# Attention of a pair in two-bank tiles, and seven products for all of batches 1 to 3

## The chip, the cores and the metric

One core of a Trainium2 chip runs the whole program in one launch. The metric is device time in microseconds (us). Engines: TensorE (PE, and PEld for its weight loads), VectorE (DVE), ScalarE (ACT), GpSimd (POOL), and SyncE (SP), whose queue issues most DMAs.

## What is computed

```python
# q, k, v: (B, H, S, D) = (4, 8, 768, 64); n_global 8, n_local 96
scores = q @ k.T / sqrt(D)
keep   = (pos_k < 8) | ((0 <= rel) & (rel < 96))        # rel = pos_q - pos_k
dist   = 96 for a global key out of the window, else |rel|
scores = where(keep, scores - slope[h] * dist, -1e9)    # slope[h] = 2 ** -(h + 1)
x      = softmax(scores) @ v                            # heads side by side: (4, 768, 512)
u      = x + (U @ V) applied along the sequence         # rank 32; U 768x32, V 32x768
out    = u + relu(u @ w_ch1) @ w_ch2                    # 512 -> 2048 -> 512
```

The slope of a head is half that of the head before it.

## The kernel before

A step `i` handles one pair of heads: `b = i // 4` is the batch, `i % 4` the pair, 16 steps in all. The instructions stand in the order in which the program writes them (a manual schedule), so every engine works off its own queue in that order.

**Attention of a pair.** Per 128 queries only their own 128 keys count (`kT`), and the 128 before with the 8 global keys patched in (`kA`). The 11 blocks of a head lie side by side, 1408 columns, made in three chunks of 512, 512 and 384 (`st_S(i, c)`, scores at L360 and L367). For batch 0 a matmul adds the bias (L352) and ScalarE takes the exponential from PSUM (`st_SE`, L379). From batch 1 on VectorE adds the bias table `relcat`, one step a head and chunk (`s_dve`, L392), from PSUM into `sp`, and ScalarE takes one exponential a head (`st_E`, L404). `st_V` multiplies by `v` (L416, L420) into the PSUM tile `ob`; VectorE takes the reciprocal of the sums (L425) and normalizes (L439); GpSimd casts to fp16 into `x16` (L440).

**Low-rank step.** `st_M1` (L449) projects `x16` on U, VectorE copies (L453); `st_MT` turns it (L466), VectorE copies it to `tmp16` (L467); `st_M3` multiplies by V (L503) in two halves of three matmuls, in an `sc` bank and in `ob`; VectorE adds each half to `x_sb` (L508), GpSimd casts the whole (L512), and `st_X` has a DMA transpose it to `uT`. Batch 0 does the add by `st_M2` instead (copies at L485 and L487).

**Feed-forward.** A batch has three groups of 256 tokens. A group has 8 *up* units of 8 matmuls of 256 columns (L609), each with a ReLU into `htr` (L614). Then a plain group has 8 *down* units of 4 matmuls of 512 columns (L639), with an add to `x_sb` and a store after each four (L644). A group in `WG` does the down projection as a 2 x 2 block product by seven block products instead of eight: units x1 to x4 in PSUM tile `cx` and y1 to y3 in `cy`, each 8 matmuls of 256 columns (L659) and a VectorE add to `x_sb` (L664). For these VectorE makes sums s1 to s4 of blocks of `htr`, in two parts each, and once sums t1 to t4 of blocks of `w_ch2` (L540). The sums wait in the list `jobs`; one is taken off after each unit, and `need` takes off what a product lacks, in order, just before it.

**Order.** A first loop (i = 0 to 3) does attention of batch 0. The second loop's passes, called slots here by their `i` (4 to 17), put feed-forward units between the pieces of attention: the tuple `units` says how many stand at each of nine places. In order: chunk 0 of pair i, 1st place, `st_V(i-1, 0)` and (i < 7) the transposes of the next pair (`st_T`, L250, kT copied at L273), 2nd, chunk 1, 3rd, `st_V(i-1, 1)`, 4th, chunk 2, 5th, `st_M1(i-1)` and the first exponential, 6th, `st_MT(i-1)` and the next pair's kA (`st_K`, L335, L336), 7th, `st_M3(i-1, 0)` and the second exponential, 8th, `st_M3(i-1, 1)` and `st_X`, 9th. Chunk 0 of slot 4 stands ahead of the loop, among the last steps of batch 0. What units are left after slot 17 run by themselves: the tail. In slots 4 to 6 the units are batch 0's ups; GpSimd also makes kA there (L290), casts v (L136), copies vA (L299) and issues weight DMAs (L222, L225).

PSUM has eight banks: two single-bank `sc` tiles, one `ob`, two `cps` (also `cx`, `cy`), three `th` (ups, transposes).

Of the kernel before, what the change touches and what calls it, by code (L numbers as in the profile page):

```python
# [20 lines left out]
def kernel(  # L21
# [46 lines left out]
    WG = ((2, 1), (2, 2), (3, 0), (3, 1), (3, 2))  # L68
# [11 lines left out]
    def ps_sc(tag="sc"):  # L80
        return psum.tile([P, 512], FP32, name="sc", tag=tag, bufs=2)
# [84 lines left out]
    setup = scp.tile([P, 384], I32, name="setup", tag="ep0")  # L166
# [16 lines left out]
    relcat = cst.tile([P, 640], FP32, name="relcat")  # L183
# [17 lines left out]
    for vt in vbuf:  # L201
        nc.gpsimd.memset(vt[:, :, :, D:D + 1], 1.0)
    nc.gpsimd.tensor_copy(relcat[:, 0:512].rearrange("p (a c) -> p a c", a=2), rel3[:, 0:2])
    nc.gpsimd.tensor_copy(relcat[:, 512:640], relB[:, 0:P])
    finish_table(
        relcat, relcat[0:NG, 0:512].rearrange("p (a c) -> p a c", a=2)[:, :, P:]
    )
# [22 lines left out]
    def new_batch(b):  # L230
        xs[b] = xp.tile([P, NSB, DM], FP32, name="x_sb", tag="x_sb", bufs=3)
        x16s[b] = xp.tile([P, NP, NSB, P], FP16, name="x16", tag="x16")
        tmps[b] = xp.tile([P, DM], FP16, name="tmp16", tag="tmp16", bufs=3)
        uTs[b] = xp.tile([P, NDC, S], FP16, name="uT", tag="uT")
# [97 lines left out]
    def st_K(i):  # L332
        kT = kts[i]
        kA = kp.tile([P, NSB - 1, P], FP16, name="kA", tag="kA")
        nc.vector.tensor_copy(kA.rearrange("d n p -> d (n p)"), kT[:, 0:S - P])  # L335
        nc.vector.tensor_copy(  # L336
            kA[:, 1:, 0:NG], kT[:, 0:NG].unsqueeze(1).broadcast_to((P, NSB - 2, NG))
        )
        kas[i] = kA
# [3 lines left out]
    def scores(i, c, on_pe):  # L343

        kT, kA, qT = kts[i], kas[i], qts[i]
        c0 = 512 * c
        tot = min(512, W - c0)
        r0 = 256 if c else 0
        scs = [ps_sc("cps" if on_pe and (i + c) % 2 else "sc") for hi in range(2)]
        if on_pe:  # L350
            for hi in range(2):
                nc.tensor.matmul(  # L352
                    scs[hi][:, 0:tot], slI[:, 2 * (i % NP) + hi],
                    rel16.rearrange("p a c -> p (a c)")[:, r0:r0 + tot], start=True, stop=False,
                )
        for kb in (2 * c, 2 * c + 1):
            o = 256 * kb - c0
            for hi in range(2):
                r = slice(hi * D, (hi + 1) * D)
                nc.tensor.matmul(  # L360
                    scs[hi][:, o:o + P], kT[r, kb * P:(kb + 1) * P], qT[r, kb * P:(kb + 1) * P],
                    start=(o == 0 and not on_pe), stop=(o + P == tot),
                )
# [7 lines left out]
        return [(sc, c0, tot, r0) for sc in scs]  # L371

    def st_SE(i, c):

        if c == 0:
            for hi in range(2):
                eps[i, hi] = scp.tile([P, W], FP16, name=f"ep{hi}", tag=f"ep{hi}")
        for hi, (sc, c0, tot, _) in enumerate(scores(i, c, True)):
            nc.scalar.activation(  # L379
                eps[i, hi][:, c0:c0 + tot], sc[:, 0:tot], AF.Exp, scale=qk_scale  # L380
            )

    relfs = (relcat[:, 0:512], relcat[:, 256:512].unsqueeze(1).broadcast_to((P, 2, 256)), relcat[:, 256:640])

    def s_dve(i, hi, got):
        sc, c0, tot, r0 = got
        if c0 == 0:
            sps[i, hi] = scp.tile([P, W], FP32, name=f"sp{hi}", tag=f"sp{hi}", bufs=1)
        dst, got = sps[i, hi][:, c0:c0 + tot], sc[:, 0:tot]
        if c0 == 512:  # L390
            dst, got = (t.rearrange("p (a c) -> p a c", a=2) for t in (dst, got))
        nc.vector.scalar_tensor_tensor(  # L392
            out=dst, in0=got,
            scalar=qk_scale / slope[2 * (i % NP) + hi], in1=relfs[c0 // 512],
            op0=ALU.mult, op1=ALU.add,
        )

    def st_S(i, c):
        for hi, got in enumerate(scores(i, c, False)):
            s_dve(i, hi, got)  # L400

    def st_E(i, hi):
        ep = scp.tile([P, W], FP16, name=f"ep{hi}", tag=f"ep{hi}")
        nc.scalar.activation(  # L404
            ep, sps.pop((i, hi)), AF.Exp, scale=slope[2 * (i % NP) + hi]
        )
        eps[i, hi] = ep

    def st_V(i, hi):
        b, h = i // NP, 2 * (i % NP) + hi  # L410
        ep, vt, vA = eps.pop((i, hi)), vts[i], vas[i]
# [15 lines left out]
        x16 = x16s[b][:, i % NP, :, hi * D:(hi + 1) * D]  # L427
# [12 lines left out]
        nc.gpsimd.tensor_copy(x16, xo)  # L440


    def st_M1(i):
        b, dc = i // NP, i % NP
        ch = slice(dc * P, (dc + 1) * P)
        if b:
            tps = ps_ob()
            for n in range(NSB):
                nc.tensor.matmul(  # L449
                    tps[:, 0:R], x16s[b][:, dc, n], u16[:, n, 0:R],  # L450
# [5 lines left out]
        for n in range(NSB):  # L456
            nc.tensor.matmul(
                tps[:, 0:P], u16[:, n], x16s[b][:, dc, n],
# [10 lines left out]
    def st_M2(i):  # L469
        b, dc = i // NP, i % NP  # L470
        ch = slice(dc * P, (dc + 1) * P)
        for g in range(2):
# [5 lines left out]
            for t in range(NTG):  # L478
                nc.tensor.matmul(
                    ups[:, t * P:(t + 1) * P], x16s[b][:, dc, NTG * g + t], ident16,  # L480
# [9 lines left out]
    def st_X(i):  # L490
# [3 lines left out]
            x16s[b][:, dc].rearrange("p n d -> p (n d)"),  # L494
        )

    def st_M3(i, g):
        b, dc = i // NP, i % NP
        ch = slice(dc * P, (dc + 1) * P)
        ups = ps_ob() if g else ps_sc()  # L500
        for t in range(NTG):
            n = NTG * g + t
            nc.tensor.matmul(  # L503
                ups[:, t * P:(t + 1) * P], v16w[:, n * P:(n + 1) * P], tmps[b][:, ch],
                start=(t == 0), stop=(t == NTG - 1),
            )
        dst = xs[b][:, NTG * g:NTG * (g + 1), ch]
        nc.vector.tensor_tensor(  # L508
            dst, ups[:, 0:GT].rearrange("p (t d) -> p t d", t=NTG), dst, ALU.add
        )  # L510
        if g == 1:
            nc.gpsimd.tensor_copy(x16s[b][:, dc], xs[b][:, :, ch])  # L512
# [23 lines left out]
    have = set()  # L536

    def queue_sum(name, part, out_, a, b_, op):
# [35 lines left out]
    def queue_group(b, g):  # L574
# [9 lines left out]
        def queue_sums(k):  # L584

            h = cell["htr"]
            if k == 0:
                for x in range(1, 5):
                    cell[f"s{x}"] = ffp.tile([P, HJ, P], FP16, name=f"s{x}", tag=f"s{x}", bufs=1)
                cell.update(a11=h[:, 0:HJ, 0:P], a12=h[:, HJ:NJC, 0:P],  # L590
                            a21=h[:, 0:HJ, P:FT], a22=h[:, HJ:NJC, P:FT])
            js = slice(k * HJ // 2, (k + 1) * HJ // 2)
            for name, a, b_, op in (
# [3 lines left out]
                queue_sum((name, b, g), k, cell[name][:, js], cell[a][:, js], cell[b_][:, js], op)  # L597
# [76 lines left out]
        if split:  # L674
# [7 lines left out]
            for made in (x1, y1, x2, y2, x3, y3, x4) if last else (x1, y1, y2, x2, y3, x3, x4):  # L682
# [8 lines left out]
    def fill(n):  # L691
        for _ in range(n):
            unit()
            if jobs:
                jobs.popleft()()
# [22 lines left out]
    for i in range(NP):  # L718
# [34 lines left out]
        if i == 2:  # L753
            load_w1(1)
        st_SE(i, 2)
# [19 lines left out]
    for i in range(NP, NPAIR + 2):  # L775
# [65 lines left out]
        if i > NP:  # L841
            st_M3(i - 1, 0)
# [3 lines left out]
        if i > NP:  # L846
            st_M3(i - 1, 1)
# [45 lines left out]
```

## Time and profile before

| | |
|---|---|
| median of 3 runs (lowest, highest) | 233.26 us (233.09, 233.36) |
| the profiled execution: its time, its span | 233.38 us, 231.4 us |
| granted TensorE clock | 0.999 |
| matmuls of plain downs (L639), of products (L659) | 224, 280 |
| bias steps of VectorE (L392), 128x512 and 128x384 | 48 and 24 |

The span runs from the first to the last instruction that the profile holds; 2.0 us of the time lie outside it. In windows, an engine's busy time is the union of its instructions' records. Matmul records overlap, since matmuls are pipelined: the time of a row of them is read from one start to the next. Slots 4 to 15 begin, at the first scores of chunk 0, at 27.4, 39.5, 50.5, 60.7, 72.4, 83.9, 96.2, 108.4, 120.4, 132.4, 144.4 and 156.5 us; the tail begins near 180.

### The profile page before, as it was taken

The numbers are of one execution on the slowest core, as the hardware profiler recorded it, in microseconds if no ns is written. First come the engines' busy times: TensorE is split into PE (matmuls) and PEld (weight loads), VectorE is DVE, ScalarE is ACT, GpSimd is POOL, SyncE is SP. The second block draws the span as 40 slices with busy tenths as digits, with TensorE's granted clock in tenths as the row PEclk, the third lists the DMA queues.
The fourth block names the chain that finished last, engine by engine and source line by source line (L and its number), as shares of the span: only waits on it lengthen the run. The fifth ranks groups of instructions, "written<-read, shape, count | busy, mean of one in ns | idle before, by whom it ended". The sixth has DMA issues, their size and how long they took to land.

```text
span 231.4 us, 5678 instructions
## 1 busy us (share of the span) xinstructions
PE 223.6 (97%) x2324; PEld 161.5 (70%) x2324; DVE 150.4 (65%) x350; ACT 111.3 (48%) x167; POOL 80.5 (35%) x131
## 2 busy tenths in 40 slices
PE   7999999999999999999999999999999999999994
PEld 2455678778644457766666756866688888888883
DVE  3787794868577767566657675779895524444452
ACT  6776948685722222927263707473533334333320
POOL 6399736668344243332415051503120100000000
PEclk9999999999999999999999999999999999999999
DMA  6999999999999997987695965542131302011112
GB/s 194 308 287 248 253 215 244 307 178 139 226 204 279 215 259 181 225 180 198 147 235 121 259 152 145 144 103 79 32 81 48 79 3 91 1 48 45 45 48 91
DMA packets 86561, 36.66 MB, mean 158 GB/s; under 512 B 74152, under 2 KB 83592, under 8 KB 86536
## 3 DMA queue, kind: packets, MB, share of 16 engines
q1 hardware_dynamic: 81480, 32.01, 54.5%
q0 software_dynamic: 5056, 4.29, 12.8%
q8 instruction: 18, 0.29, 0.6%
q14 instruction: 7, 0.06, 0.1%
HBM read 27.46 MB, written 6.29 MB: 146 GB/s over the span
## 4 chain that ended last, share of the span: by engine, by line
PE 83%; POOL 5%; DMA 3%; DVE 3%; ACT 2%; issue 1%; SPq 1%; POOLq 0%
PE hps L609 33%; PE cps L639 22%; PE cx L659 8%; PE cy L659 5%; PE sc L360 3%; DMA vst<-in_v_dram 3%; PE ob L420 2%; PE ob L416 2%; PE sc L367 1%; ACT ep L404 1%; POOL v L136 1%; PE sc L503 1%; ACT htr L614 1%; PE ob L503 1%; PE tp L250 1%
## 5 line engine op out<-in xcount | busy, mean ns | idle before, releaser
L614 ACT ACTIVATE htr<-hps 128x512 f16<-128x512 f32 x96 | 56.8, 598 | 85.3 <-PE hps L609 82.4
L609 PE MATMUL hps<-uT,w 128*128 128x256 f16 x756 | 96.2, 273 | 0.5 <-DVE uT L485 0.3
L609 PEld LDWEIGHTS <-w 128*128 128x128 f16 x756 | 70.5, 98 | 11.3 <-issue 0.4
L639 PE MATMUL cps<-w,htr 128*128 128x512 f16 x224 | 56.9, 379 | 0.0
L392 DVE SCALAR_TENSOR_TENSOR sp<-sc,relcat 128x512 f32<-128x512 f32 (+1 forms) x72 | 43.2, 640 | 17.6 <-PE sc L360 8.9
L404 ACT ACTIVATE ep<-sp 128x1408 f16<-128x1408 f32 x24 | 32.7, 1372 | 16.3 <-DVE sp L392 16.3
L512 POOL CAST x<-x_sb 128x768 f16<-128x768 f32 x12 | 10.3, 856 | 61.9 <-DVE x_sb L508 61.9
L639 PEld LDWEIGHTS <-htr 128*128 128x128 f16 x224 | 19.1, 97 | 16.6
L440 POOL CAST x<-x_sb 128x384 f16<-128x384 f32 x30 | 15.8, 526 | 25.8 <-DVE x_sb L439 25.6
L360 PEld LDWEIGHTS <-kT 64*128 64x128 f16 x192 | 8.2, 93 | 15.1 <-issue 13.5
L540 DVE TENSOR_TENSOR s<-htr 128x512 f16<-128x512 f16 x20 | 9.3, 463 | 12.7 <-ACT htr L614 12.7
L439 DVE TENSOR_TENSOR x_sb<-ob,rcp 128x384 f32<-128x384 f32 x30 | 16.7, 557 | 1.0
L659 PEld LDWEIGHTS <-s 128*128 128x128 f16 x160 | 15.5, 98 | 1.8
L360 PE MATMUL sc<-qT,kT 64*128 64x128 f16 x192 | 16.8, 221 | 0.0
L420 PE MATMUL ob<-v,ep 128*128 128x65 f16 x192 | 16.5, 193 | 0.0
L420 PEld LDWEIGHTS <-ep 128*128 128x128 f16 x192 | 13.9, 98 | 3.0 <-ACT ep L379 0.3
L664 DVE TENSOR_TENSOR x_sb<-cx,x_sb 128x256 f32<-128x256 f32 x20 | 8.4, 422 | 10.1 <-PE cx L659 10.0
L416 PE MATMUL ob<-vA,ep 128*128 128x65 f16 x160 | 14.4, 194 | 0.4 <-DVE vA L312 0.2
L136 POOL CAST v<-vst 128x768 f16<-128x768 f32 x16 | 13.5, 842 | 3.6 <-DMA vst<-in_v_dram 3.6
L367 PE MATMUL sc<-qT,kA 64*128 64x128 f16 x160 | 14.2, 217 | 0.4 <-DVE kA L286 0.2
L379 ACT ACTIVATE ep<-sc 128x512 f16<-128x512 f32 (+1 forms) x24 | 12.1, 559 | 4.4 <-PE sc L367 4.1
L659 PEld LDWEIGHTS <-htr 128*128 128x128 f16 x120 | 11.7, 98 | 1.3
(102 smaller groups left out, 265.7 us busy)
## 6 DMA issues: line engine op xcount, KB each, us to landing
qst<-in_q_dram SPq DMA_DIRECT2D x16, 384.0 KB, 4.7
kst<-in_k_dram SPq DMA_DIRECT2D x16, 384.0 KB, 6.7
vst<-in_v_dram SPq DMA_DIRECT2D x16, 384.0 KB, 3.8
out_dram<-x_sb SPq DMA_DIRECT2D x23, 256.0 KB, 2.3
w<-in_moe_w_ch_dram POOLq DMA_DIRECT2D x8, 512.0 KB, 8.0
vA<-v SPq DMA_DIRECT2D x8, 152.3 KB, 4.4
out_dram<-x_sb SPq DMA_DIRECT2D x2, 128.0 KB, 1.7
uT<-x SPq DMA_TRANSPOSE x12, 2.8
```

What stands on the lines that cost most here:

```text
L136: nc.gpsimd.tensor_copy(vt.rearrange("p n h d -> p h n d")[:, :, :, 0:D], vsts.pop(i).rearrange("p (h n) d -> p h n d", h=2),)
L360: nc.tensor.matmul(scs[hi][:, o:o + P], kT[r, kb * P:(kb + 1) * P], qT[r, kb * P:(kb + 1) * P], start=(o == 0 and not on_pe), stop=(o + P ...
L367: nc.tensor.matmul(scs[hi][:, o + P:o + 2 * P], kA[r, kb], qT[r, (kb + 1) * P:(kb + 2) * P], start=False, stop=(o + 2 * P == tot),)
L392: nc.vector.scalar_tensor_tensor(out=dst, in0=got, scalar=qk_scale / slope[2 * (i % NP) + hi], in1=relfs[c0 // 512], op0=ALU.mult, op1=ALU ...
L404: nc.scalar.activation(ep, sps.pop((i, hi)), AF.Exp, scale=slope[2 * (i % NP) + hi])
L416: nc.tensor.matmul(ob[:, qi], ep[:, OF[qi - 1]:OF[qi - 1] + P], vA[:, qi - 1, hi], start=True, stop=False,)
L420: nc.tensor.matmul(ob[:, qi], ep[:, DG[qi]:DG[qi] + P], vt[:, qi, hi], start=(qi == 0), stop=True,)
L439: nc.vector.tensor_tensor(xo, ob[:, :, 0:D], rb, ALU.mult)
L609: nc.tensor.matmul(hps[:, k * FT:(k + 1) * FT], w1_16[:, dc, jt * P:(jt + 1) * P], uT[:, dc, ts], start=(dc == 0 and k == 0), stop=(dc == ...
L614: nc.scalar.activation(cell["htr"][:, 2 * jp:2 * jp + 2].rearrange("p j t -> p (j t)"), hps, AF.Relu)
L639: nc.tensor.matmul(cps, htr[:, jc, t * P:(t + 1) * P], w2_16[:, jc], start=(b > 0 and jc == 0), stop=(jc == NJC - 1),)
L659: nc.tensor.matmul(ps, cell[a][:, j], tw[w][:, j], start=(first and j == 0), stop=(done is not None and j == HJ - 1), skip_group_check=True,)
```

## The change

- `WG` holds all nine groups of batches 1 to 3 (five before). The products of every group stand in the order x1, y1, x2, y2, x3, y3, x4, so `cx` and `cy` take turns.
- The `sc` tile is one tile of two banks, one copy: a bank a head. VectorE's bias step covers both heads in one instruction: the table `relcat2` holds the table and its half, and the scale is that of the pair's first head. `sp` and `ep` are pair tiles. In batch 0 every second chunk has one exponential for both heads, the others use two `cps` tiles. `st_R` makes the half table in pass 2 of the first loop.
- `st_M3` is one block of six matmuls in the two banks of `sc`, with one VectorE add.
- Chunk 0's bias step of slot 4 is issued after the last `st_M2` of batch 0; before, its two steps stood between the pieces ahead of it.
- The large part of the kA copy (L335 before) goes to ScalarE.
- s3 is made in place of a block of `htr`. The weight sums t1, t2, t4 have a buffer of their own and start in group (0, 1). Every sum carries a count of units before which it isn't taken off the list; `need` ignores the count.
- `units`: slots 4 to 6 move the unit of the 3rd place to the 9th (8 units as before); slots 7 and 8 have 9 instead of 10, slots 9 to 17 10 instead of 11.

```diff
-    WG = ((2, 1), (2, 2), (3, 0), (3, 1), (3, 2))
+    WG = tuple((b, g) for b in range(1, B) for g in range(NFG))
...
-    def ps_sc(tag="sc"):
-        return psum.tile([P, 512], FP32, name="sc", tag=tag, bufs=2)
+    def ps_sc():
+        return psum.tile([P, 2, 512], FP32, name="sc", tag="sc", bufs=1)
...
-        nc.vector.tensor_copy(kA.rearrange("d n p -> d (n p)"), kT[:, 0:S - P])
+        nc.scalar.copy(kA[:, :, NG:], kT.rearrange("d (n p) -> d n p", n=NSB)[:, 0:NSB - 1, NG:])
...
-        scs = [ps_sc("cps" if on_pe and (i + c) % 2 else "sc") for hi in range(2)]
+        both = None if on_pe and (i + c) % 2 else ps_sc()
+        scs = [ps_cps("sc") if both is None else both[:, hi] for hi in range(2)]
...
+    def st_R():
+        nc.vector.tensor_scalar_mul(relcat2[:, 1], relcat, 0.5)
+    relfs = (relcat2[:, :, 0:512], relcat2[:, :, 256:768], relcat2[:, :, 256:640])
...
         nc.vector.scalar_tensor_tensor(
-            out=dst, in0=got,
-            scalar=qk_scale / slope[2 * (i % NP) + hi], in1=relfs[c0 // 512],
+            out=sps[i][:, :, c0:c0 + tot], in0=both[:, :, 0:tot],
+            scalar=qk_scale / slope[2 * (i % NP)], in1=relfs[c0 // 512],
             op0=ALU.mult, op1=ALU.add,
         )
...
-    def st_M3(i, g):
-        ups = ps_ob() if g else ps_sc()
+    def st_M3(i):
+        ups = ps_sc()
...
-    def queue_sum(name, part, out_, a, b_, op):
+    def queue_sum(name, part, out_, a, b_, op, wait=0):
...
-        jobs.append(go)
+        jobs.append((count[0] + wait, go))
...
-        t = xp.tile([P, 3, HJ, HD], FP16, name="t16", tag="x_sb", bufs=3)
+        t = wbig.tile([P, 3, HJ, HD], FP16, name="t16")
...
-                queue_sum(name, k, tw[name][:, js], a[:, js], b_[:, js], ALU.subtract)
+                queue_sum(name, k, tw[name][:, js], a[:, js], b_[:, js], ALU.subtract, wait=4 * len(jobs))
...
-                            a21=h[:, 0:HJ, P:FT], a22=h[:, HJ:NJC, P:FT])
+                            a21=h[:, 0:HJ, P:FT], s3=h[:, 0:HJ, P:FT], a22=h[:, HJ:NJC, P:FT])
...
-                queue_sum((name, b, g), k, cell[name][:, js], cell[a][:, js], cell[b_][:, js], op)
+                queue_sum((name, b, g), k, cell[name][:, js], cell[a][:, js], cell[b_][:, js], op, wait=0 if last else 2)
...
-                if (t, part) == (0, 1) and not split and follow in WG:
+                if (t, part) == (0, 1) and (b, g) == (0, NFG - 2):
                     queue_weight_sums()
...
-            for made in (x1, y1, x2, y2, x3, y3, x4) if last else (x1, y1, y2, x2, y3, x3, x4):
+            for made in (x1, y1, x2, y2, x3, y3, x4):
...
     def fill(n):
         for _ in range(n):
             unit()
-            if jobs:
-                jobs.popleft()()
+            count[0] += 1
+            if jobs and jobs[0][0] < count[0]:
+                jobs.popleft()[1]()
...
     st_M2(NP - 2)
-    s_dve(NP, 0, first[0])
     begin_up(0, (0, 1), ps_cps("hps"))
     st_M1(NP - 1)
-    s_dve(NP, 1, first[1])
     begin_up(0, (2,))
     begin_up(1, (0, 1, 2), ps_th("hps"))
     st_M2(NP - 1)
+    s_dve(NP, first)
...
-            (1, 1, 1, 1, 1, 1, 1, 1, 0) if i + 1 < NPE
-            else (1, 1, 1, 2, 1, 1, 1, 1, 1) if i < 2 * NP + 1
-            else (2, 1, 1, 2, 1, 1, 1, 1, 1)
+            (1, 1, 0, 1, 1, 1, 1, 1, 1) if i + 1 < NPE
+            else (1, 1, 1, 1, 1, 1, 1, 1, 1) if i < 2 * NP + 1
+            else (1, 1, 1, 2, 1, 1, 1, 1, 1)
```

More of the change, by code (lines that the diff above doesn't have):

```diff
@@ L165 @@
     warm(8)
-    setup = scp.tile([P, 384], I32, name="setup", tag="ep0")
+    setup = scp.tile([P, 384], I32, name="setup", tag="ep")
     reli = setup[:, 0:256]
@@ L182 @@
     nc.vector.tensor_copy(ident16, ident)
-    relcat = cst.tile([P, 640], FP32, name="relcat")
+    relcat2 = cst.tile([P, 2, 768], FP32, name="relcat")
+    relcat = relcat2[:, 0]
     rel16 = cst.tile([P, 3, 256], BF16, name="rel16")
@@ L202 @@
         nc.gpsimd.memset(vt[:, :, :, D:D + 1], 1.0)
[L203 to L207, printed above, removed]
+    relcat3 = relcat.rearrange("p (a c) -> p a c", a=3)
+    nc.gpsimd.tensor_copy(relcat3, rel3)
+    finish_table(relcat, relcat3[0:NG, :, P:])
     def load_uv():
@@ L370, in scores, with s_dve @@
                     )
-        return [(sc, c0, tot, r0) for sc in scs]
+        return scs, both, c0, tot
     def st_SE(i, c):
         if c == 0:
-            for hi in range(2):
-                eps[i, hi] = scp.tile([P, W], FP16, name=f"ep{hi}", tag=f"ep{hi}")
-        for hi, (sc, c0, tot, _) in enumerate(scores(i, c, True)):
+            eps[i] = scp.tile([P, 2, W], FP16, name="ep", tag="ep")
+        scs, both, c0, tot = scores(i, c, True)
+        if both is not None:
             nc.scalar.activation(
-                eps[i, hi][:, c0:c0 + tot], sc[:, 0:tot], AF.Exp, scale=qk_scale
+                eps[i][:, :, c0:c0 + tot], both[:, :, 0:tot], AF.Exp, scale=qk_scale
             )
-    relfs = (relcat[:, 0:512], relcat[:, 256:512].unsqueeze(1).broadcast_to((P, 2, 256)), relcat[:, 256:640])
-    def s_dve(i, hi, got):
-        sc, c0, tot, r0 = got
+            return
+        for hi, sc in enumerate(scs):
+            nc.scalar.activation(
+                eps[i][:, hi, c0:c0 + tot], sc[:, 0:tot], AF.Exp, scale=qk_scale
+            )
+    def st_R():
+        nc.vector.tensor_scalar_mul(relcat2[:, 1], relcat, 0.5)
+    relfs = (relcat2[:, :, 0:512], relcat2[:, :, 256:768], relcat2[:, :, 256:640])
+    def s_dve(i, got):
+        _, both, c0, tot = got
         if c0 == 0:
[L388 to L391, printed above, removed]
+            sps[i] = scp.tile([P, 2, W], FP32, name="sp", tag="sp", bufs=1)
         nc.vector.scalar_tensor_tensor(
-            out=dst, in0=got,
-            scalar=qk_scale / slope[2 * (i % NP) + hi], in1=relfs[c0 // 512],
+            out=sps[i][:, :, c0:c0 + tot], in0=both[:, :, 0:tot],
+            scalar=qk_scale / slope[2 * (i % NP)], in1=relfs[c0 // 512],
             op0=ALU.mult, op1=ALU.add,
@@ L398, in st_S @@
     def st_S(i, c):
-        for hi, got in enumerate(scores(i, c, False)):
-            s_dve(i, hi, got)
+        s_dve(i, scores(i, c, False))
     def st_E(i, hi):
-        ep = scp.tile([P, W], FP16, name=f"ep{hi}", tag=f"ep{hi}")
+        if hi == 0:
+            eps[i] = scp.tile([P, 2, W], FP16, name="ep", tag="ep")
         nc.scalar.activation(
-            ep, sps.pop((i, hi)), AF.Exp, scale=slope[2 * (i % NP) + hi]
+            eps[i][:, hi], sps[i][:, hi], AF.Exp, scale=slope[2 * (i % NP)]
         )
-        eps[i, hi] = ep
     def st_V(i, hi):
         b, h = i // NP, 2 * (i % NP) + hi
-        ep, vt, vA = eps.pop((i, hi)), vts[i], vas[i]
+        ep, vt, vA = eps[i][:, hi], vts[i], vas[i]
+        if hi == 0:
+            x16s[i] = xp.tile([P, NSB, P], FP16, name="x16", tag="x16", bufs=3)
         obf = ps_cps("ob") if (i, hi) == (NP - 1, 1) else ps_ob()
@@ L426, in st_V @@
         xo = xs[b][:, :, h * D:(h + 1) * D]
-        x16 = x16s[b][:, i % NP, :, hi * D:(hi + 1) * D]
+        x16 = x16s[i][:, :, hi * D:(hi + 1) * D]
         rb = rcp.unsqueeze(2).broadcast_to((P, NSB, D))
@@ L493, in st_X @@
             uTs[b][:, dc].rearrange("d (n p) -> d n p", n=NSB),
[L494 removed]
+            x16s[i].rearrange("p n d -> p (n d)"),
         )
[L497 removed]
+    def st_M3(i):
         b, dc = i // NP, i % NP
         ch = slice(dc * P, (dc + 1) * P)
[L500 to L502 removed]
+        ups = ps_sc()
+        for n in range(NSB):
+            g, t = divmod(n, NTG)
             nc.tensor.matmul(
[L504 removed]
+                ups[:, g, t * P:(t + 1) * P], v16w[:, n * P:(n + 1) * P], tmps[b][:, ch],
                 start=(t == 0), stop=(t == NTG - 1),
             )
[L507 removed]
+        dst = xs[b][:, :, ch].rearrange("p (g t) d -> p g t d", g=2)
         nc.vector.tensor_tensor(
[L509 removed]
+            dst, ups[:, :, 0:GT].rearrange("p g (t d) -> p g t d", t=NTG), dst, ALU.add
         )
[L511 to L512 removed]
+        nc.gpsimd.tensor_copy(x16s[i], xs[b][:, :, ch])
     ups_q, downs_q = deque(), deque()
@@ L754 @@
             load_w1(1)
+            st_R()
         st_SE(i, 2)
@@ L841 @@
         if i > NP:
-            st_M3(i - 1, 0)
+            st_M3(i - 1)
         if live:
@@ L846 @@
         if i > NP:
-            st_M3(i - 1, 1)
             st_X(i - 1)
```

14 lines of the change are left out of this document (7 added, 7 removed).

## The prediction

> **What bounds the kernel now.** I read the page first, then busy time in windows (one per slot, from the first scores of one slot to those of the next), the chain of waits in order of time, and the timeline around the places that the change touches. A lane is an engine's queue, which it works off in order.
>
> ```profile
> PE 223.6 (97%) x2324; PEld 161.5 (70%) x2324; DVE 150.4 (65%) x350; ACT 111.3 (48%) x167; POOL 80.5 (35%) x131
> ```
> ```profile
> 39.51:50.54 11.03, 10.61 (x135) 8.60 (x135) 7.37 (x15) 8.49 (x13) 7.61 (x12) 1.00 1.15 247
> 108.41:120.41 12.00, 12.00 (x122) 7.83 (x121) 7.79 (x17) 6.19 (x8) 4.16 (x7) 1.00 0.74 173
> 156.47:167.50 11.03, 11.03 (x118) 7.42 (x118) 10.06 (x23) 5.01 (x7) 3.21 (x4) 1.00 0.22 58
> ```
> After the stretch and its length come busy PE, PEld, DVE, ACT and POOL. TensorE is busy throughout in slot 11 and in slot 15 up to its `st_M3` (second and third line), at full clock. VectorE has 4.2 us to spare in slot 11, but 1.0 us in slot 15, where weight sums and the first product sums fall. So TensorE's work is the time, unless a wait is put into its lane.
>
> ```profile
> 84.65 1.73 PE cps L639 x8
> ```
> ```profile
> 224.57 0.87 PE cy L659 x8
> 225.45 0.87 PE cx L659 x8
> ```
> From the chain: eight 512-column matmuls of a plain down take 1.73 us (0.216 each); eight 256-column matmuls of a product take 0.87 (0.109 each).
>
> **A. Four more groups by seven products.** A plain group's down projection is 32 x 0.216 = 6.92 us, one by products 7 x 0.87 = 6.11: 0.8 saved. The order in which the changed program stands has 504 product matmuls against 280 and 96 plain ones against 224, so four groups: **-3.2**. All of it is on TensorE, which sets the end. Fewer units in a slot only move units to the tail, where the same lane does them.
>
> The Trainium skill ("TensorE: Matmul & The Clock Gate", Back-to-back issue gap) gives 81 ns for a 128-column and 131 ns for a 512-column matmul in a stream with weight loads. By that a plain unit would be 4 x 0.131 = 0.52 and, estimated at about 0.1 per 256 columns, a product 0.8, so that the four groups would cost about 6 us instead of saving 3. The 0.216 and 0.109 above disagree, and the sum goes by them.
>
> **B. Slots 4 to 6: the bias step of a pair.** Before, a head's step (L392) frees its own bank. Now one step covers both banks of the only `sc` tile, so the next scores wait for all of it. Its size: 512 columns take 0.684 and 384 take 0.551 (mean of the groups), 1.04 ns a column, so 1024 take 0.684 + 0.53 = 1.22 and 768 take 0.95 (ends: 0.68, one step, and 1.37, two). Steps in a row overlap by some 0.08.
>
> ```profile
> 31.43 0.56 DVE L485 CAST uT<-ups 128x384 f16<-128x384 f32 x1 [0.22 <-PE ups L479]
> 31.90 1.01 DVE L772 TENSOR_TENSOR x_sb<-ob,rcp 128x384 f32<-128x384 f32 x2
> 33.13 0.96 DVE L273 COPY kT<-tp 128x768 f16<-128x768 f16 x1 [0.21 <-PE tp L250]
> 34.00 1.28 DVE L392 SCALAR_TENSOR_TENSOR sp<-sc,relcat 128x512 f32<-128x512 f32 x2
> ```
> ```profile
> 33.79 1.91 PE L609 MATMUL hps<-uT,w 128*128 128x256 f16 x16 [0.16 <-ACT qT L272]
> 35.63 0.23 PE L360 MATMUL sc<-qT,kT 64*128 64x128 f16 x2
> ```
> Slot 4, timeline of before. Chunk 0's two steps ran at 29.74 and 30.54, ahead of the last uT copy. The change issues its one step behind that copy, from 31.90. Queued behind it on VectorE: two L772 (0.93), kT (0.87), then chunk 1's step: 31.90 + 1.13 + 0.93 + 0.87 = 34.83, done 36.05. TensorE waits for it: between scores 1 and 2 there is now one unit, not two (33.79 + 0.97 = 34.76). Scores 2 start at 36.1: a wait of **1.3**.
>
> ```profile
> 45.11 0.85 POOL L136 CAST v<-vst 128x768 f16<-128x768 f32 x1
> 46.03 0.73 POOL L299 COPY vA<-v 128x650 f16<-128x650 f16 x1
> 46.70 0.51 POOL L440 CAST x<-x_sb 128x384 f16<-128x384 f32 x1
> ```
> ```profile
> 47.27 0.22 PEld L449 LDWEIGHTS <-x 128*128 128x128 f16 x6 [0.62 <-POOL x L440]
> ```
> Slots 5 and 6: `st_M1` needs GpSimd's second x16 cast, which stands behind kA (43.44), a weight DMA, v and vA, some 3.8 us from kT's end. TensorE already waits 0.5 there in slot 5. ScalarE's second exponential ends near 41.65 by the shift; the pair's chunk-0 step, whose output tile both exponentials read, follows at 41.7, then two steps and kT (to 44.5); the cast ends 1.1 later than before. TensorE arrives a unit (0.87) earlier in its slot, so 1.1 + 0.87 = 2.0 lost by the end of slot 5, that is 0.6 beyond slot 4. In slot 6, where the cast ended (57.06) only 0.34 ahead of its reader, 0.87 - 0.34 = 0.5 and 0.1 at scores 2: 0.6. B is **+2.5**; ends 0.7 (the waits of 0.5 and 0.4 that slot 5 has now absorb the shift) and 3.2.
>
> **C. The first group of batch 1, slot 10.** There its first s1, s2, s4, s3 and the last weight sums meet. TensorE's order is six low-rank matmuls, product x2 (t2 by s2), up; VectorE's is the low-rank add (`st_M3`), s1, s2, and x2's fifth weight load waits for that s2. The merged add is 0.555 + 384 x 1.04 ns = 0.95. From the end of M3's stream: 0.27 (94.17 to 94.44, first half's add of before), 0.87, s1 0.34, s2 0.42, signal and load 0.17 = 2.07; TensorE wants it 0.44 after that end. **+1.6**; ends 0 (s1 and s2 would have to run ahead of the add, which the order denies) and 2.0.
>
> **D. Other waits in slots 9 to 16.** VectorE there, back to back: steps 1.13 + 1.13 + 0.87, two reciprocals and normalizations 1.4, small copies 0.5, low-rank add 0.87 = 5.9; four to six sums at 0.34 and four or five product adds at 0.34 make 8.9 to 9.6. TensorE's slot is 10 x 0.873 and 2.63 of attention (12.24 of slot 10 less 11 units) = 11.4. So VectorE fits except in slot 10 (5.9 + 1.0 + 8 x 0.34 + 3 x 0.6 = 11.4). Laid out, TensorE meets a late copy at `st_MT` or `st_M3` for 0.2 to 0.35 in slots 9, 10, 11, 13, 14 and 16, as at 105 us now, where an L644 add stands ahead of the copy L467 and M3 comes 0.2 late: 1.7. From 89 to 180 us the blocks of TensorE's lane now start 1.5 later in all than their columns take; that goes. **+0.2**, ends -1 and +2.
>
> **E. Small ones.** The halved table (`st_R`): one 768-column step in a lane full from 20 to 26 us; nearest row the L122 cast of as many, 0.55; behind its place some 0.3 to 0.5 of the lane is idle before 26 us: +0.1, ends 0 and 0.4. The kA copy (L335, 0.32) moves to ScalarE (near L272: 0.80 for 768 columns, so 0.6), between the exponentials; ScalarE has over 5 of 12 us free and the next pair's step comes 0.75 ahead of its reader: 0, or 0.2 a slot if that cover is gone. GpSimd's table copies come before 10.4, where it waits 3.6 for v. SP's order is unchanged; weight sums into a buffer of their own free an `x_sb`, which nobody waits for. Merged exponentials save some 0.1 each off the path: 0 (ends -0.3, +0.3).
>
> **F. Two engines at one memory.** A sum alone takes 0.41, but one that starts beside a GpSimd cast (POOL L512 at 169.48, 0.83 long):
>
> ```profile
> 169.60 0.98 DVE L540 TENSOR_TENSOR s<-htr 128x512 f16<-128x512 f16 x1
> ```
> Of 12 sums in live slots two were stretched, by 0.9 in all. Some 40 will now stand there: 2.9 us of VectorE, mostly into its slack of 2 a slot. **+0.3**, ends 0 and 3. The Trainium skill ("GPSIMD Engine Reference", Key points) says that GpSimd shares its SBUF interfaces with VectorE, and names instructions with two SBUF inputs. The row agrees; of the rules I found it speaks most against this change.
>
> **Sum.** -3.2 + 2.5 + 1.6 + 0.2 + 0.1 + 0.3 = +1.5, on the profiled execution's own 233.38 (span 231.4 and 2.0 around it): 234.9; that run lies 0.12 over the median of 233.26, so **234.8** for a median.
>
> **Rivals.**
> - *Faster: GpSimd keeps up.* If the x16 casts of slots 5 and 6 are ready when TensorE arrives, B is 0.7 and the sum -0.3; with C also halved, 232.1. For it: slot 6 had 0.34 to spare, and slot 15 bore 91% of VectorE without TensorE falling idle. Against: a unit is taken out ahead of that very cast. It decides at the end of the second cast, 46.9 on before's clock. Without any new wait the floor is A alone, 230.1. Chance 0.22.
> - *The terms cancel* (about 233.3): B and C together at half. 0.10.
> - *VectorE becomes the bound in slots 9 to 16*: stretched sums over 2 us a slot. If every sum in a slot took the 0.98 of the row under F, 5 x 0.57 = 2.9 a slot are 0.9 past the slack; over six slots, 5 on top of the sum: 240. Within slower, 0.12.
> - *Weight loads bind the short matmuls*: 24 more loads a group, 96 x 0.098 = 9.4 us if they showed. 244; the tail's products at 0.109 with loads of 98 ns beside them deny it. The Trainium skill's rule under A leans that way. Within slower, 0.01.
> - *The change doesn't do what it says*: denied by the counts in its order.
>
> **How the numbers follow.** Forecast 0.55, the two slow rivals 0.13, cancel 0.10, faster 0.22. A fifth of a per cent (0.5 us) is about what can be told from no change. The range reaches down to B 0.7, C 0.4 and no F, -1.8 (231.5), and up to B 3.2, C 2.0, F 1.0 and D 0.8, +3.9 (237.2): each side leaves about a tenth.
>
> **What would show it.** Scores 2 of slot 4 waiting over 1 us for VectorE; `st_M1` of slots 5 and 6 waiting for the x16 cast, 1.4 and 0.5; one product load of about 1.6 behind s2 in slot 10, right after M3; the pair's step at 1.22; products at 0.87 from there to the end. If slot 7's first scores come under 61.9 (60.66 now), B is wrong; if x2 runs on without a break, C is.

## The result, and the profile after

| | before | after |
|---|---|---|
| median (lowest, highest) | 233.31 us (233.09, 234.0) | 236.45 us (235.9, 240.39) |
| the profiled execution: time, span | 233.38, 231.4 us | 236.29, 234.5 us |

After to before is 1.0122, 95% interval 1.0089 to 1.0154: slower by 1.2%, or 2.8 us. This leaves out the run of 240.39, whose mean granted clock was 0.992; the median without it is 236.29. The prediction was 234.8. Line numbers from here on are those of the changed kernel.

The first line of the page after:

```profile
PE 221.4 (94%) x2418; PEld 170.9 (73%) x2420; DVE 161.8 (69%) x347; ACT 115.3 (49%) x169; POOL 83.5 (36%) x130
```

TensorE is busy for 2.2 us less than before although the time is longer: it waits. Windows show where (stretch and its length, then busy PE, PEld, DVE, ACT and POOL, the granted clock, DMA share, GB/s): slots 5, 10, 11, and 15 up to its `st_M3`.

```profile
41.66:53.23 11.57, 10.38 (x134) 8.51 (x134) 7.50 (x12) 8.58 (x13) 6.99 (x11) 1.00 1.17 250
97.05:110.68 13.63, 11.64 (x137) 9.24 (x136) 11.89 (x24) 7.27 (x11) 7.65 (x9) 1.00 0.90 193
110.68:122.16 11.48, 11.41 (x138) 9.33 (x139) 9.33 (x21) 6.01 (x9) 2.48 (x4) 1.00 0.83 200
156.44:167.40 10.96, 10.96 (x137) 9.37 (x137) 9.72 (x20) 5.67 (x8) 2.58 (x5) 1.00 0.16 35
```

Slot 10 is 2.15 us longer than slot 11 with as many matmuls (137 and 138), and TensorE idles for 2.0 of them. Slot 15 is full, as before.

The two groups whose size the prediction had to estimate (count, then busy us and mean ns of one, then idle time before them), and a product in the chain of waits:

```profile
L398 DVE SCALAR_TENSOR_TENSOR sp<-sc,relcat 128x1024 f32<-128x1024 f32 x24 | 29.3, 1221 | 7.5 <-PE sc L367 3.2 <-ACT ep L410 2.4 <-issue 1.2
L515 DVE TENSOR_TENSOR x_sb<-sc,x_sb 128x768 f32<-128x768 f32 x12 | 11.5, 956 | 4.8 <-PE sc L510 4.8
```
```profile
115.79 0.87 PE cy L667 x8
```

They are 1.22, 0.96 and 0.87, as worked out (1.22, 0.95, 0.87). What was to be shown by the timeline, slots 4 to 6:

```profile
32.25 0.56 DVE L492 CAST uT<-ups 128x384 f16<-128x384 f32 x1 [0.91 <-PE ups L486]
32.72 1.22 DVE L398 SCALAR_TENSOR_TENSOR sp<-sc,relcat 128x1024 f32<-128x1024 f32 x1
33.85 1.01 DVE L781 TENSOR_TENSOR x_sb<-ob,rcp 128x384 f32<-128x384 f32 x2
34.78 0.95 DVE L272 COPY kT<-tp 128x768 f16<-128x768 f16 x1
35.65 1.22 DVE L398 SCALAR_TENSOR_TENSOR sp<-sc,relcat 128x1024 f32<-128x1024 f32 x1
...
36.91 0.23 PE L360 MATMUL sc<-qT,kT 64*128 64x128 f16 x2 [1.27 <-DVE sp L398]
...
49.09 0.32 PE L456 MATMUL ob<-u,x 128*128 128x32 f16 x6 [1.19 <-POOL x L447]
...
59.78 0.32 PE L456 MATMUL ob<-u,x 128*128 128x32 f16 x6 [0.32 <-POOL x L447]
```

The queue on VectorE is the one laid out: the pair's step behind the last uT copy, two late normalizations, kT, the next step. Scores 2 of slot 4 wait 1.27 for it, and `st_M1` of slots 5 and 6 waits 1.19 and 0.32 for the second x16 cast. And slot 10:

```profile
106.69 0.60 PE L667 MATMUL cx<-t,s 128*128 128x256 f16 x4
106.96 0.96 DVE L515 TENSOR_TENSOR x_sb<-sc,x_sb 128x768 f32<-128x768 f32 x1 [0.24 <-PE sc L510]
107.83 0.42 DVE L548 TENSOR_TENSOR s<-htr 128x512 f16<-128x512 f16 x1
107.98 0.96 POOL L518 CAST x<-x_sb 128x768 f16<-128x768 f32 x1 [4.40 <-DVE x_sb L515]
108.28 0.93 DVE L548 TENSOR_TENSOR s<-s,htr 128x512 f16<-128x512 f16 x1
...
109.27 0.61 PE L667 MATMUL cx<-t,s 128*128 128x256 f16 x4 [1.98 <-DVE s L548]
```

Product x2 stops after four of eight matmuls and waits 1.98 for s2, which stands behind the low-rank add. s2 itself takes 0.93 for 0.42: the add has just released GpSimd's cast, which runs beside it. From the start of x2 to the start of the next unit it takes 3.02 instead of 0.87, so 2.15 are lost.

**The account**, from the starts of slots and the last matmul's end (231.20 after, 228.07 before, 3.1 apart): slot 4 starts 0.8 later; slots 4 to 6 take 35.74 instead of 33.30, +2.4; from slot 7 to the end 167.28 instead of 167.41, -0.1.

### The profile page after: what moved, and what is told of

Same layout as the page of the kernel before. It is cut to its first block, busy times and chain, and to the rows that moved or that the text cites. A ratio compares the mean times of both kernels' runs of the same rounds, so it can differ in the third digit from the quotient of the medians.

```text
span 234.5 us, 5851 instructions
## 1 busy us (share of the span) xinstructions
PE 221.4 (94%) x2418; PEld 170.9 (73%) x2420; DVE 161.8 (69%) x347; ACT 115.3 (49%) x169; POOL 83.5 (36%) x130
## 4 chain that ended last, share of the span: by engine, by line
PE 53%; DVE 4%; issue 0%; DVEq 0%
PE hps L617 24%; PE cx L667 13%; PE cy L667 10%; PE sc L360 2%; PE sc L510 1%; DVE s L548 1%; DVE x_sb L672 1%; PE ob L427 1%; PE ob L423 1%; DVE x_sb L515 1%; PE sc L367 1%; DVE sp L398 0%; PE ob L456 0%; DVE tmp L474 0%; DVE htr L548 0%
## 5 line engine op out<-in xcount | busy, mean ns | idle before, releaser
L398 DVE SCALAR_TENSOR_TENSOR sp<-sc,relcat 128x1024 f32<-128x1024 f32 (+1 forms) x36 | 40.7, 1131 | 8.7 <-PE sc L367 3.2
L667 PEld LDWEIGHTS <-htr 128*128 128x128 f16 x288 | 27.3, 98 | 3.2
L672 DVE TENSOR_TENSOR x_sb<-cx,x_sb 128x256 f32<-128x256 f32 x36 | 15.2, 422 | 19.7 <-PE cx L667 19.5
L447 POOL CAST x<-x_sb 128x384 f16<-128x384 f32 x30 | 16.8, 560 | 30.8 <-DVE x_sb L446 30.6
L647 PE MATMUL cps<-w,htr 128*128 128x512 f16 x96 | 24.3, 379 | 0.0
L667 PEld LDWEIGHTS <-s 128*128 128x128 f16 x216 | 20.5, 98 | 4.9 <-DVE s L548 2.3
L672 DVE TENSOR_TENSOR x_sb<-cy,x_sb 128x256 f32<-128x256 f32 x27 | 11.4, 422 | 12.4 <-PE cy L667 12.2
L360 PEld LDWEIGHTS <-kT 64*128 64x128 f16 x192 | 8.7, 93 | 15.0 <-issue 13.5
L667 PE MATMUL cx<-w,htr 128*128 128x256 f16 x144 | 18.7, 273 | 0.0
L515 DVE TENSOR_TENSOR x_sb<-sc,x_sb 128x768 f32<-128x768 f32 x12 | 11.5, 956 | 4.8 <-PE sc L510 4.8
```

The source lines that it names most:

```text
L360: nc.tensor.matmul(scs[hi][:, o:o + P], kT[r, kb * P:(kb + 1) * P], qT[r, kb * P:(kb + 1) * P], start=(o == 0 and not on_pe), stop=(o + P ...
L398: nc.vector.scalar_tensor_tensor(out=sps[i][:, :, c0:c0 + tot], in0=both[:, :, 0:tot], scalar=qk_scale / slope[2 * (i % NP)], in1=relfs[c0 ...
L647: nc.tensor.matmul(cps, htr[:, jc, t * P:(t + 1) * P], w2_16[:, jc], start=(b > 0 and jc == 0), stop=(jc == NJC - 1),)
L667: nc.tensor.matmul(ps, cell[a][:, j], tw[w][:, j], start=(first and j == 0), stop=(done is not None and j == HJ - 1), skip_group_check=True,)
L672: nc.vector.tensor_tensor(x_sb[:, n, cs], ps, x_sb[:, n, cs], ALU.add)
```

## The experiments

Eleven kernels, each an edit of the changed one, beside runs of the kernel before on the same chip (its medians there: 233.09 for e1 to e4, 233.42 for e5 to e8, 233.53 for e9 to e11). Three stretches of the profile say more than the times: slots 4 to 6, slot 10, and slot 7 to the end. For up to slot 4 these kernels are nearly the same program, yet slot 4 starts between 26.9 and 28.3 in their profiles. Most of that arises before pass 3 of the first loop, whose first scores start between 21.3 and 22.9. So a time of one run can't tell 1 us; lengths of slots can tell 0.1. The columns: median time; ratio to the kernel before with its interval; lengths of slots 4, 5, 6 and their sum; length of slot 10; slot 7 to the last matmul.

| | median | ratio (95%) | slots 4, 5, 6 | sum | slot 10 | slot 7 to end |
|---|---|---|---|---|---|---|
| before | 233.31 | | 12.15, 11.03, 10.12 | 33.30 | 12.24 | 167.4 |
| after | 236.45 | 1.0122 (1.0089, 1.0154) | 13.48, 11.57, 10.69 | 35.74 | 13.63 | 167.3 |
| e1 units back | 236.42 | 1.0129 (1.0088, 1.017) | 12.61, 11.88, 10.43 | 34.92 | 14.53 | 168.8 |
| e2 step back | 236.24 | 1.0134 (1.01, 1.0168) | 12.98, 11.57, 10.68 | 35.23 | 13.83 | 169.3 |
| e3 both | 236.07 | 1.0131 (1.0098, 1.0163) | 12.47, 11.86, 10.44 | 34.77 | 13.64 | 167.3 |
| e4 weight sums early | 234.92 | 1.0076 (1.0051, 1.0101) | 13.48, 11.56, 10.68 | 35.72 | 11.48 | 166.6 |
| e5 five groups | 236.04 | 1.0118 (1.0093, 1.0143) | 13.49, 11.55, 10.68 | 35.72 | 11.17 | 167.8 |
| e6 weight sums every 3 | 233.75 | 1.0019 (0.9998, 1.004) | 13.48, 11.55, 10.68 | 35.71 | 11.48 | 165.3 |
| e7 v behind the cast | 241.37 | 1.0338 (1.0287, 1.0388) | 13.49, 15.01, 11.28 | 39.78 | 13.63 | 167.6 |
| e8 cast on ScalarE | 236.07 | 1.012 (1.0095, 1.0146) | 13.48, 11.55, 10.69 | 35.72 | 13.49 | 167.4 |
| e9 step, v, patch | 231.65 | 0.9925 (0.99, 0.9949) | 12.98, 10.32, 10.32 | 33.62 | 11.48 | 165.5 |
| e10 and half table | 232.61 | 0.997 (0.9945, 0.9995) | 12.99, 10.32, 10.32 | 33.63 | 11.48 | 166.1 |
| e11 and units back | 232.38 | 0.9946 (0.9924, 0.9968) | 12.47, 10.82, 10.43 | 33.72 | 11.48 | 166.7 |

### Term B: the step's place and the units (e1, e2, e3)

```diff
-            (1, 1, 0, 1, 1, 1, 1, 1, 1) if i + 1 < NPE     # e1, e3
+            (1, 1, 1, 1, 1, 1, 1, 1, 0) if i + 1 < NPE
...
     st_M2(NP - 2)                                          # e2, e3
+    s_dve(NP, first)
     begin_up(0, (0, 1), ps_cps("hps"))
...
     st_M2(NP - 1)
-    s_dve(NP, first)
```

> Only the unit of slots 4 to 6 goes back from the 9th to the 3rd place; the merged step stays behind the last uT copy. Theory (the step's place and the missing unit add up): scores 2 of slot 4 start at the same time, as VectorE sets them, but TensorE waits 0.4 there instead of 1.27; the x16 casts end where they did and TensorE comes to them at the same time, so the waits of st_M1 in slots 5 and 6 stay near 1.2 and 0.3. Gain 0.87: 235.4 us. Rival (the unit's place is all of B): both kinds of wait go, 2.4 gained, 233.9. Rival (the unit covers nothing, the waits move with it): 236.3.

> Only the merged bias step of chunk 0 of slot 4 goes back to where the first head's step stood, ahead of the last st_M1 of batch 0; units as in the change. Theory: no wait at scores 2 of slot 4 (1.27 gained); the second x16 cast of slot 5 ends some 1.1 earlier but TensorE comes 1.27 earlier too, so its wait stays at 1.2 to 1.4. 235.1 us. Rival (the step, not the unit, is what the casts wait for, and TensorE is not early): all of B goes, 233.9. Rival (the step delays the uT copies, and TensorE waits there instead): 236.3.

> Both of these edits. Theory: they add, 1.27 + 0.87 = 2.1 gained, st_M1 of slot 5 waits 0.5 as in the kernel before, 234.2 us, and slot 7 starts at 61.7 instead of 63.9. Rival (merging the two heads in one tile costs by itself, since scores 2 wait for a step of 1.22 instead of 0.68): 235 or more, with a wait at scores 1 or 2 left in slots 4 to 6.

Measured by the three slots: the units are worth 0.82 (0.87 expected), the step's place 0.51 (1.27 expected), both 0.97 (2.1 expected). In e2 scores 2 of slot 4 still wait 0.44 for chunk 1's step, as one tile serves all chunks, and the step in its old place delays the pieces behind it by 0.3. So the gains don't add, and with both edits in 1.5 of B stays. The medians of the three, 236.1 to 236.4, missed what was expected (234.2 to 235.4); the last section says why. The profile of e3 beside that of the kernel before shows what stays. In e3 the first exponential of the previous pair ends at 38.82, the second at 41.06:

```profile
37.45 1.37 ACT L410 ACTIVATE ep<-sp 128x1408 f16<-128x1408 f32 x1
...
39.67 1.39 ACT L410 ACTIVATE ep<-sp 128x1408 f16<-128x1408 f32 x1
...
41.09 1.23 DVE L398 SCALAR_TENSOR_TENSOR sp<-sc,relcat 128x1024 f32<-128x1024 f32 x1 [2.75 <-ACT ep L410]
```

And in the kernel before, whose line of this step is L392:

```profile
40.01 0.69 DVE L392 SCALAR_TENSOR_TENSOR sp<-sc,relcat 128x512 f32<-128x512 f32 x1 [2.22 <-PE sc L367]
41.12 0.69 DVE L392 SCALAR_TENSOR_TENSOR sp<-sc,relcat 128x512 f32<-128x512 f32 x1 [0.43 <-ACT ep L404]
```

The pair's step of slot 5 has one `sp` tile to write, which both exponentials read, so it starts at 41.09 behind the second. Before, the first head's own `sp` tile was free, and its step ran at 40.01, where only the second head's waited. So the step of chunk 0 ends 0.5 later (42.32 against 41.81), the x16 cast too (47.70 against 47.21), and `st_M1` waits 0.86 where it waited 0.34. Besides, with no unit in the 9th place chunk 0 of the next slot waits 0.24 for the low-rank add (L515), since both now use the one `sc` tile, which makes slots 5 and 6 0.3 longer each; and in slot 4 the step of 1.22, ahead of `st_M1`'s copy on VectorE, makes `st_M2` 0.3 late. 0.5 + 0.3 + 0.3 + 0.3 = 1.4, about the 1.5 that stays. This is read from the two profiles; no run gave the pair a second `sp` or `sc` tile.

### Term C: the sums ahead of slot 10 (e4, e6)

```diff
-... ALU.subtract, wait=4 * len(jobs))
+... ALU.subtract)                          # e4
+... ALU.subtract, wait=3 * len(jobs))      # e6
```

> The weight sums t1, t2, t4 lose their count of units, so that they come one a unit in slots 7 and 8; the first product group's s1 and s2 then stand ahead of the low-rank add of slot 10 on VectorE. Theory C (the order on VectorE makes the break of 2.15 in x2): the break goes, 234.1 us, and slots 7 to 9 lose at most 0.3 to the denser sums. Rival (slot 10 is full on VectorE and the break only moves to the next sum or product): 235.8 to 236.3, with a wait of 1 to 2 elsewhere in slots 10 and 11. Rival (the denser sums delay the bias steps of slots 7 and 8): a new wait of some 1 us at scores there.

> As the run with early weight sums, but a weight sum may come off the list every 3 units (every 4 in the change, at once in that run), so that at most one stands ahead of a normalization in each slot and all stand ahead of slot 10's first products. Theory (the break of 2.15 in slot 10 is the place of s1 and s2; the 1.3 that the early sums lost at st_M1 of slot 8 is their crowding ahead of a normalization): both are gone, 236.3 - 2.15 - 0.1 = 234.0 us, and no stretch of lower granted clock in slot 10, since TensorE does not fall idle there. Rival (VectorE has no room, the time comes back in slots 8 to 10): 235.

Both take the break out: slot 10 has 11.48. But in e4 1.5 comes back in slot 8, through denser sums as in the last rival, though not at the scores: in its profile `st_M1` there waits 1.14 for the x16 cast, because three weight sums stand ahead of that pair's second normalization on VectorE in this slot (one in the change). At one every 3 units neither wait is there, and slot 7 to the end is 2.0 shorter than in the change. C is shown: the break came from the place of s1 and s2 in VectorE's order, and one digit of pacing gets back 2.0 of its 2.15.

### Terms A and F (e5, e8)

```diff
-    WG = tuple((b, g) for b in range(1, B) for g in range(NFG))     # e5
+    WG = ((2, 1), (2, 2), (3, 0), (3, 1), (3, 2))
...
     def st_M3(i):                                                   # e8
...
-        nc.gpsimd.tensor_copy(x16s[i], xs[b][:, :, ch])
...
     def st_X(i):
...
+        nc.scalar.copy(x16s[i], xs[b][:, :, dc * P:(dc + 1) * P])
```

> The changed kernel with the old WG: four of the nine groups plain again (down by 512-column matmuls), everything else as in the change. Theory (term A, 0.8 a group on TensorE's lane; the break of 2.15 in slot 10 goes with the groups of batch 1): 236.3 + 3.2 - 2.15 = 237.3 us, and from the start of slot 11 to the end some 2.4 us more than in the changed kernel (three groups' worth of A). Rival (products gain nothing, as the loads and sums eat it): 234.1. Rival (the four groups brought sums that slow VectorE by more than A): under 234.

> The cast of x16 after the low-rank add goes from GpSimd to ScalarE, behind the second exponential, for all pairs. Theory F (sums are stretched because a GpSimd cast runs beside them): from slot 10 on hardly a sum of 512 columns over 0.45 is left that stands behind a low-rank add; the break in slot 10 shrinks by the 0.5 that s2 was stretched, 2.15 to 1.65, and 235.6 us. Rival (sums are stretched by something else, DMA writes say): as many stretched sums as before, 236.3. Rival (ScalarE's later ReLUs and exponentials hold up TensorE): 237 or more, waits for htr or for the sp tile.

A: e5's time of 236.04 lies between the 237.3 expected and the rival's 234.1 and doesn't decide. But e5 and e6 are both without the break and differ by four groups, and e6's median, from the same round, is 2.3 lower. From the start of slot 10 to the last matmul e5 takes 134.66 (97.13 to 231.79), e6 132.00 (95.89 to 227.89), 2.7 less; e6's late copies hold it up 1.4 there, e5's 1.0, which leaves 3.1 for the four groups, against 3.2 worked out. By the Trainium skill's rule under A ("TensorE: Matmul & The Clock Gate", Back-to-back issue gap) they would have cost an estimated 6; the traces contradict it.

F: of the change's 72 half sums eleven take over 0.45, 3.3 us too much in all, and each runs beside a GpSimd cast; those with 0.65 or more of one cast beside them take 0.92 to 1.01 for 0.42. Each of the eleven ends 0.27 after the cast that was running when it began, however much of that cast was left. The five sums that began ahead of a cast kept 0.42, and it was the cast that grew (0.96 for 0.83, 0.64 for 0.51). So in these traces the instruction that comes second waits for the first; the two don't just slow each other. In e8 s2 takes 0.43 and the break of 2.15 is 1.64, as expected. But the time gained hardly anything (236.07, slot 10 at 13.49): another s2 of slot 10 was stretched to 0.95 beside GpSimd's k cast, which no longer stood behind the x16 cast in that queue and so came 5 us earlier, and `st_MT` waited 0.47 behind that s2. Nine sums were still stretched, each beside another cast.

### Making room for the cast (e7, e9, e10, e11)

```diff
-        if live:
+        if live and not NP < i < NPE:
             cast_v(i)
             st_A(i)
...
             st_V(i - 1, 1)
+        if NP < i < NPE:
+            cast_v(i)
+            st_A(i)
+            st_P(i, nc.gpsimd)      # e9, e10, e11; in e7 st_P stays on VectorE at chunk 2
...
     finish_table(relcat, relcat3[0:NG, :, P:])                    # e10
+    nc.gpsimd.tensor_scalar_mul(relcat2[:, 1], relcat, 0.5)       # in place of st_R()
```

e9 to e11 also have e2's place of the step and e6's weight sums, e11 e1's units.

> In slots 5 to 7 GpSimd's v cast and vA copy are issued behind st_V(i-1, 1) and so behind the second x16 cast; bias step, units and sums as in the change. Theory (st_M1 of slots 5 and 6 waits only for that cast, which stands 1.6 behind v and vA): the waits of 1.19 and 0.32 go, with 0.4 of start-to-start time around them 1.36 + 0.49 = 1.85 gained; slot 4's wait of 1.27 stays. Slot 7 starts 33.9 after slot 4 instead of 35.7, 234.5 us. Rival (the cast is late because the step and the normalization ahead of it on VectorE are): the cast ends 0.5 earlier at most, 235.8.

e7 was a miss by 7 us: 241.37 where 234.5 was expected. Slots 4 to 6 took 4.0 longer than in the change, and all its runs show a lower granted clock besides (0.979 to 0.993). From its timeline:

```profile
49.19 2.40 DVE L311 COPY vA<-v 8x520 f16<-8x520 f16 x1 [1.32 <-POOL vA L298]
51.51 0.17 DVE L460 CAST zw<-ob 128x32 f16<-128x32 f32 x1
...
51.74 0.29 PE L473 MATMUL ob<-ident,zw 128*128 128x128 f16 x1 [2.91 <-DVE zw L460]
```

The cast came 1.2 earlier in its slot, as meant, and `st_M1` didn't wait. But VectorE's patch of vA (`st_P`) stands ahead of `st_M1`'s copy in VectorE's lane; it now waited 1.32 for the later vA and, beside GpSimd's q and k casts (49.84 to 51.43), took 2.40 instead of 0.56. The wait was moved from one lane to the next and grew.

> Weight sums every 3 units; the bias step of slot 4 back at its old place; in slots 5 to 7 v cast and vA copy behind the second x16 cast, and the patch of vA (L311, 0.56 to 2.40 on VectorE) made by GpSimd right behind vA. Theory (the run with v behind the cast lost 3 us only because VectorE's patch, which stands ahead of st_M1's copy, then waited for vA and ran beside a GpSimd cast): no wait of TensorE over 0.3 at st_M1 or st_MT in slots 5 and 6, slot 7 starts 33.4 after slot 4 (35.7 in the change, 33.3 before), and 231.4 us, under the kernel before by 0.8%. Rival (GpSimd has no room for the patch too, and its queue runs late for the next kA or x16): 233 or more.

> The kernel with step, v and patch moved, and besides the half table made by GpSimd in the setup, where it waits for v, instead of by VectorE in pass 2. Theory (the early 0.8 by which slot 4 started later in the change is partly st_R: 0.54 on VectorE beside a slow q cast, 0.5 at the transposes of pair 3): slot 4 starts 0.5 earlier than in the kernel without this edit, 230.9 us. Rival (the start of slot 4 differs between runs by as much, 27.0 to 28.2 so far, for other reasons): no difference that can be told.

> The kernel with step, v and patch moved, and the units of slots 4 to 6 as before (one in the 3rd place, none in the 9th). Theory (with the cast early the unit in the 3rd place only covers 0.4 of waits in slot 4, while the 9th place's unit covers the merged low-rank add, which holds the pair's sc tile: 0.41 in each of slots 5 and 6 without it): slot 7 starts 33.8 after slot 4, 0.4 later than without this edit, 231.8 us. Rival (the 3rd place's unit covers more, as in the prediction's term of 0.87): 230.6.

e9 has the patch on GpSimd, right behind vA:

```profile
46.62 0.51 POOL L447 CAST x<-x_sb 128x384 f16<-128x384 f32 x1 [0.35 <-DVE x_sb L446]
47.07 0.85 POOL L137 CAST v<-vst 128x768 f16<-128x768 f32 x1
47.98 0.73 POOL L298 COPY vA<-v 128x650 f16<-128x650 f16 x1
48.77 0.61 POOL L311 COPY vA<-v 8x520 f16<-8x520 f16 x1
...
47.19 0.32 PE L456 MATMUL ob<-u,x 128*128 128x32 f16 x6
```

`st_M1` doesn't wait for it, slots 4 to 6 take 33.62 (33.4 expected), and the median is 231.65 (231.12 to 232.27): it beats both kernels, the one before by 0.75% (0.51 to 1.0). The moves of the step, of v and of the patch were not run one by one. With the units back (e11) slot 4 gains 0.5 and slot 5 loses 0.5 again, 0.3 of it to the low-rank add: no difference there.

e10 shows the price of `st_R`. From pass 3's first scores to slot 4 every kernel with it takes 5.53 to 5.55, the kernel before 5.07, e10 5.06. With it GpSimd's q cast, which runs beside, takes 1.36 in ten kernels and 1.08 in the change, against 0.89 in the kernel before and in e10, and the k transposes of pair 3 wait 0.26 for the k cast behind it. So `st_R` costs 0.48 in that place, shown by taking it out of VectorE's lane there; e10's median of 232.61 (230.9 expected) is still no better than e9's. In its profiled run TensorE lost 0.7 within an up in slot 9, 0.5 of it waiting for the DMA that turns `uT` (0.2 lost in e9). That does not come from this edit alone: e11, without it, waits 0.64 there for the same DMA and 0.47 for the one that writes vA, and its slot 9 is 1.2 longer than e9's, which is all that its stretch from slot 7 to the end is longer. Why those transfers land late in some runs is open.

## Why the prediction was right or wrong

Right: slower, by the mechanisms named, at the places named. Too low, by sizes: from the first instruction to the last the profiled execution grew by 3.1 where 1.5 was forecast, and the median without the run of 240.39 is 1.5 over the prediction.

- **A, -3.2**: 3.1 by e5 against e6. A product takes 0.87, as before, with its loads beside it.
- **B, +2.5**: 2.44, and slot 7 starts at 63.9, past the 61.9 set as the test. The waits were those listed. But its split fails, so that the total is partly luck: step and units together account for 1.0, and the rest is the pair tiles themselves, `sp` with one copy and `sc` shared with the low-rank add. The prediction named the tile that both exponentials read, but charged slots 5 and 6 with 0.87 each for the unit taken out ahead of the cast. With the unit put back (e1) these two slots take 22.31, against 22.26 in the change: its wait only moved.
- **C, +1.6**: 2.15. The term was mis-sized at s2, put at 0.42. F's own mechanism, a sum beside a GpSimd cast, struck here, on the path: the low-rank add releases the cast and the sum together. It was priced as a mean over all sums, when the order showed that this sum always has that neighbour.
- **D and F, +0.5**: what is left of slot 7 to the end after A and C is 167.28 - 167.41 + 3.1 - 2.15 = 0.8. TensorE is held up 0.2 to 0.3 in each of slots 9, 10, 11, 13, 14 and 16, as said, in slot 9 at the next scores, else at `st_M3`; outside slot 10 no stretched sum is waited for by TensorE.
- **E, +0.1**: 0.48 for `st_R` alone. What failed is the step that priced it as time in VectorE's lane and looked for idle time behind it. What it delayed was GpSimd's cast beside it, one engine over. The remaining 0.3 before slot 4 is within what that start differs by between runs.
- **kA on ScalarE, 0**: nothing waits for it (0.68, eight times).
- **Rivals.** GpSimd did not keep up: the second cast of slot 5 ended at 49.03, 48.2 on the clock of before, against the 46.9 that decides. The terms did not cancel. VectorE is not the bound: 9.33 of 11.48 in slot 11.

## What to carry to other kernels

Merging two heads into one tile halves the instructions and also halves the tiles that can be free: ask of each merged tile who frees its second half, before counting what the merged instruction saves. Before moving work in one engine's queue, look at what stands behind its reader in the other engine's queue: in e7 a cast 1.2 earlier made three slots 4 us longer through a patch of 8 partitions. A change that loses at its seams can still be right: three moves in the order, one copy on another engine and one digit of pacing turned 1.2% slower into 0.75% faster.

## What had not been expected of the hardware

The break in slot 10 has a second price in some runs. In e2 TensorE falls idle for as long as in the run shown of after, and then (windows, granted clock as the number ahead of the last two):

```profile
107.00:108.00 1.00, 0.00 (x0) 0.00 (x0) 0.97 (x3) 0.73 (x1) 0.85 (x1) 1.00 1.28 281
...
109.00:110.00 1.00, 1.00 (x9) 0.58 (x6) 0.92 (x2) 0.00 (x0) 0.84 (x2) 0.79 1.07 170
110.00:111.00 1.00, 1.00 (x12) 0.63 (x12) 0.67 (x3) 0.60 (x1) 0.00 (x0) 0.50 0.46 75
...
112.00:113.00 1.00, 1.00 (x15) 0.88 (x13) 0.42 (x1) 0.00 (x0) 0.00 (x0) 0.50 1.29 140
113.00:114.00 1.00, 1.00 (x14) 0.71 (x13) 0.75 (x2) 0.00 (x0) 0.03 (x1) 1.00 0.51 108
```

TensorE is idle from 106.46 to 108.43; from 109.58 its clock is halved, for 3.4 us (0.42 of the stretch at 109, then three whole ones), and a product takes 1.68 instead of 0.87. Slots 10 and 11 of e2 take 26.65 together against 25.11 in the profile of after: 1.5 more. The profiled execution of after had the same break at full clock throughout, so the same idle time does or doesn't trip it.

The clock records tell which. Between its changes the clock holds for whole multiples of 3.413 us: 30, 1 and 36 of them in e1 and in e2, 14, 1 and 54 in e7. Counted off in windows of that length from the first change, the break lies within one window in e1 and e2, and the clock is halved from the end of that window. In after a window's edge at 108.10 cuts the break into 0.8 and 1.2, in e3 likewise, and the clock stays. Over all 13 profiles three windows hold 1.98 us or more of idle time (e1, e2, and slot 5 of e7 with 2.83), and half a clock follows each; none follows a window with 1.71 or less. What lies between was not measured.

A mean granted clock of 0.992 or 0.993, which three or more runs of each of e1, e2 and e3 show, is what this leaves in a run. e7, whose slot 5 idles 2.91, shows 0.993 or less in all six. No run of e4, e5, e6, e9 or e11, which have no break in slot 10, nor of e8, whose break is 1.48 of idle time, has less than 0.998. Two of e10's twelve do (0.990 and 0.993) without that break; no profile shows why. The half clock is much of why e1 to e3 shortened slots 4 to 6 and gained hardly any time: the one run of e3 at full clock took 234.14, the other six 235.86 to 236.47, and the runs of e1 and e2 at 0.998 or more took 235.6 in the mean, the others 236.8 and 236.6. The Trainium skill ("TensorE: Matmul & The Clock Gate", Part 1) describes such a halving, as coming after a whole idle window of some 3.4 us of a free-running counter; the length of the half clock agrees with that, but here 2.0 us of idle time were enough.
